# A gated mix of linear attention and a GEGLU on one core: three edits to a schedule written out by hand

## The chip, the cores and the metric

One core of a Trainium2 chip runs the whole program. The metric is the time of one execution in microseconds (us), the median of several runs. The core's engines each work through their own list of instructions in order: TensorE (PE, matmuls; its weight loads are shown apart as PEld), VectorE (DVE), ScalarE (ACT) and GpSimd (POOL). SyncE (SP) has a list that holds only DMA issues; ACT issues a few DMAs too. An instruction that waits holds up everything behind it in its list.

## The reference

The input x has S = 2048 tokens of D = 576 numbers; there are H = 32 heads of 18, and the hidden width of the feed-forward part is 4608.

```python
def _A_ref(x, wqkv, wo):                    # linear attention
    q, k, v = ...                           # from x @ wqkv
    phi = lambda t: jnp.where(t > 0, t + 1, jnp.exp(t)) + 1e-6
    pq, pk = phi(q), phi(k)
    kv = jnp.einsum("bhsd,bhse->bhde", pk, v)
    z = jnp.einsum("bhsd->bhd", pk)
    num = jnp.einsum("bhqd,bhde->bhqe", pq, kv)
    den = jnp.einsum("bhqd,bhd->bhq", pq, z)[..., None] + 1e-6
    return (num / den) ... @ wo
def _B_ref(x, w_gate, w_up, w_down):        # GEGLU
    h = _gelu(x @ w_gate) * (x @ w_up)
    return h @ w_down
g = _sigmoid((x * gate_w).sum(-1, keepdims=True))
return g * _A_ref(x, wqkv, wo) + (1 - g) * _B_ref(x, w_gate, w_up, w_down)
```

## The kernel before

**Numbers.** Matmuls run on fp32r operands. To keep float32 accuracy each operand is split in a high part (`ACTIVATE Copy` to fp32r on ACT) and the rest (a subtraction on DVE or POOL), and three of the four products of the parts are added in the same PSUM bank.

**Seven products in place of eight.** The three matrix products of the GEGLU go by 2x2 blocks with the seven products of Strassen's scheme. It needs four sums of blocks of x (S1 to S4, called x sums below), four of the weights (T1 to T4) and four of h.

**Stages of the program, in order of time.**

- Up to about 133 us: the key projection of 16 tiles of tokens (t = 0 to 15), its grams, and, in the gaps, the weights of queries (`w_part`, L150), of the first gate and up block (`Early`, stored to `wp_d`) and the x sums of the second half of the tokens: six pieces k, loaded to a buffer `xu` (`ahead_load`), summed on POOL (`ahead_sums`, L281), stored to `xsum_d` (`ahead_store`, L295).
- Up to about 286 us: states, queries (`query`, L414), denominators (`den`, L554, fed by `halves_of`, L544 and L545), their reciprocals by way of DRAM (`reciprocal` stores `rden_d`, L627; `reciprocals_load` brings it back spread over the heads, L631), `scale` (L643) and the output mixing (`mixed`, L662), whose result goes to `ga_d`.
- Up to 1108 us: 36 chains of gate and up products (`gu_steps`; the list is `CHAINS`). A chain is (p, n, m): half p of the tokens, block n of 18 of the hidden width, gate or up. It has 7 steps `s1`, `s6`, `s7`, `s5`, `s2`, `s4`, `s3`; each is a product of 7 matmuls (L798) followed by what DVE and ACT do with its bank. The first chain has the order s1, s6, s2, s7, s5, s4, s3, and its first four steps run inside the attention stage. There are eight banks, so PE may run ahead of DVE by a few products only. Chains are numbered c0, c1, ... below; c0 and c1 are gate and up of (0, 0), c2 and c3 of (0, 1), c4 is the gate of (1, 1), the first on the second half of the tokens; LAST-1 and LAST are the gate and up of (1, 0).
- To the end: the down product, 84 units of 36 matmuls (`unit`, L1066), whose banks DVE adds to accumulators `acc` (L1074). The accumulators start as the attention part, loaded from `ga_d` (`acc_load`, L1043). Blocks of h come back from DRAM (`h_load`, L967) and are split (`h_make`: ACT L972, DVE L973) into five buffers `hb`; blocks of the down weights are split by `d_make` (ACT L952, POOL L954) and summed by `d_sum` (POOL L959).

**Weights of a gate or up block.** `w_fetch` loads the raw block into `wraw` and makes the four sums T in `tsum` (POOL, L806); `wraw` and `tsum` are parts of one tile `stage`. `w_split`, a chain later, splits both into `W[m]` (tiles `wg`, `wu`) in two pieces: ACT L811, POOL L812 and L813, each for `wraw` and then for `tsum`; after it the next `w_fetch` is issued.

**What DVE does in a gate chain.** `s6` and `s7` make u2 and u3 (L847, L861), blocks 3, 2 and 1 are made by L833 and go through a gelu on ACT (L823); `s2` is a gelu straight from the bank (L853 for later chains). In an up chain L836 and L826 make h, and L875, L876, L877, L887 its sums, stored to `h_d` by SP (L829). `s1` copies its bank to p1 on ACT (L842); the next chain's p1 copy comes behind this chain's gelus in ACT's list, and the u2 of that chain waits for it.

**The order.** It is a schedule written out by hand: nothing reorders it. What is not a product is hung on the (chain, step) after which it is issued, by tables: `X_AT` (x parts from `xop_d`), `S_AT` (x sums k = 0 to 5: `s_make` splits a piece by ACT L988 and L989, which is on DVE for k < 4; `s_load` loads the next but one into the same half of the tile `f`, L983), `D_AT` and `H_AT`:

```python
    S_AT = [(0, 5), (1, 0), (2, 2), (2, 5), (3, 0), (3, 3)]
    H_AT = [(LAST - 1, 3), (LAST - 1, 6)]
            ...
            if (c, i) in H_AT:
                j = H_AT.index((c, i))
                h_make(j)
                h_load((2, 3)[j])
```

`stage` also holds the raw down weights (`draw`) of the last stage. Raw blocks of h arrive in `hraw` (two places before the down stage: a part of `xo` and `e123`).

Of the kernel before, what the change touches and what calls it, by code (L numbers as in the profile page):

```python
# [8 lines left out]
F32 = mybir.dt.float32  # L9
# [29 lines left out]
def tile_gated_mix(ctx, tc, xt, xs, xn, wk, wv, wq, wo, wgu, wdn, cst, out):  # L39
# [9 lines left out]
    xop_d = dram.tile([128, 3, 5, BS], F32, name="xop_d")  # L49
    xsum_d = [dram.tile([128, 4, 256], F32, name=f"xsum_d{k}") for k in range(6)]  # L50
    ga_d = [dram.tile([128, D], F32, name=f"ga_d{i}") for i in range(NST)]
    wp_d = [dram.tile([128, 7, 5, 128], F32, name=f"wp_d{m}") for m in range(2)]
    h_d = [[dram.tile([128, 7, 3, BS], F32, name=f"h_d{p}_{i}") for i in range(NF2 // 3)] for p in range(NP)]

# [218 lines left out]
    def do(n=1):  # L273
        for _ in range(n):
            todo.popleft()()
            load()

    def sum_blocks(raw, eng):
        a11, a12, a21, a22 = (raw[:, i] for i in range(4))
        eng.tensor_tensor(a22, a21, a22, OP.add)  # L280
        eng.tensor_tensor(a21, a11, a21, OP.subtract)  # L281
        eng.tensor_tensor(a11, a22, a11, OP.subtract)
        eng.tensor_tensor(a12, a12, a11, OP.subtract)
# [7 lines left out]
    def ahead_sums(k):  # L291
        sum_blocks(ahead[k], nc.gpsimd)

    def ahead_store(k):
        nc.sync.dma_start(xsum_d[k], ahead.pop(k))  # L295

    class Early:


# [9 lines left out]

        def make(self, part):  # L310
            if part < 2:
                b12, b11, b21, b22 = (self.raw[:, i] for i in range(4))
                t1, t2, t3, t4 = (self.sums[:, i] for i in range(4))
                for o, a, b in ((t1, b12, b11), (t2, b22, t1), (t3, b22, b12), (t4, b21, t2))[2 * part:2 * part + 2]:
                    nc.gpsimd.tensor_tensor(o, a, b, OP.subtract)
                return
            i, src = ((slice(0, 3), self.raw[:, 1:4]), (slice(3, 7), self.sums))[part - 2]
            nc.scalar.activation(self.hi[:, i], src, AF.Copy)
            if self.kt < 2:
                nc.gpsimd.tensor_tensor(self.lo[:, i], src, f32(self.hi[:, i]), OP.subtract)  # L320
            else:
                nc.gpsimd.tensor_tensor(self.hi[64:96, i], src[64:96], f32(self.hi[64:96, i]), OP.subtract)
            if part == 3:
                nc.sync.dma_start(wp_d[self.m][:, :, self.kt], f32(self.hi))
                if self.kt < 2:
                    nc.sync.dma_start(wp_d[self.m][:, :, 3 + self.kt], f32(self.lo))
# [32 lines left out]
    for t in range(FIRST, NST):  # L359
# [10 lines left out]
        for k, kt in enumerate((2, 3, 4) if t % 2 else (0, 1)):  # L370
# [3 lines left out]
            if k == (t == NST - 1):  # L374
                k_split(t)
                if now:
                    now.make(2)
                elif t == NST - 3:
                    ahead_sums(0)
                elif t == NST - 1:  # L380
                    ahead_sums(1)
                    ahead_store(0)
            if k == 1:
                xn_split(t)
# [304 lines left out]
    query(0, 0)  # L689
    query(0, 1)  # L690
    ahead_store(5)
    nc.sync.dma_start(xop_d[:, A22], f32(x_slot(3, 1)))
    den(3, 0)
    halves_of(3, 2)
    den(3, 1)
    halves_of(3, 3)
    query(0, 2)
    token_load(1)
    den(3, 2)
    halves_of(3, 4)  # L700
    den(3, 3)
    scaled(2, 0)
    query(0, 3)
    den(3, 4)
    scaled(2, 1)
    mixed(2, 0)
    reciprocals(3)
    query(0, 4)
    scaled(2, 2)
    token_sums(0, 0)  # L710
    mixed(2, 1)
# [2 lines left out]
    scaled(2, 3)  # L714
    token_sums(0, 1)
    query(1, 0)
    mixed(2, 2)
    den(0, 0)
    halves_of(0, 2)
# [80 lines left out]

    def w_fetch(n, m):
        nc.sync.dma_start(wraw, wgu[n, m])
        b12, b11, b21, b22 = (wraw[:, i] for i in range(4))
        t1, t2, t3, t4 = (tsum[:, i] for i in range(4))
        for o, a, b in ((t1, b12, b11), (t2, b22, t1), (t3, b22, b12), (t4, b21, t2)):
            nc.gpsimd.tensor_tensor(o, a, b, OP.subtract)  # L806

    def w_split(m):
        w = W[m]
# [104 lines left out]
    stage = stages.tile([128, 4320], F32, name="stage")  # L914
    e123 = stages.tile([128, 3, BS], F32, name="e123")
    wraw, tsum = (stage[:, c:c + 1536].rearrange("p (i k c) -> p i k c", i=4, k=3) for c in (0, 1536))
    w_fetch(1, 0)
    bothp = both.pool("both")
    X[1] = bothp.tile([128, 7, 5, BS], F32R, name="xo2")
    es += [e123[:, i] for i in range(3)]  # L920
# [52 lines left out]
            nc.vector.tensor_tensor(h[:, 1], raw, f32(h[:, 0]), OP.subtract)  # L973

    X_AT = {(0, 5): A11, (2, 2): A12, (3, 2): A22}
    S_AT = [(0, 5), (1, 0), (2, 2), (2, 5), (3, 0), (3, 3)]

    def s_raw(k):
        return f[:, k % 2 * 2:k % 2 * 2 + 2].rearrange("p a (b c) -> p (a b) c", b=2)
# [10 lines left out]

    for k in range(2):
        s_load(k)
    LAST = len(CHAINS) - 1
    D_AT = {(LAST - 2, 0): lambda: d_make(0, 0), (LAST - 2, 4): lambda: d_sum(T1), (LAST - 1, 0): lambda: d_sum(T2),
            (LAST - 1, 2): lambda: d_make(0, 1), (LAST - 1, 4): lambda: d_make(0, 2), (LAST - 1, 6): lambda: d_sum(T3),
            (LAST, 1): lambda: d_make(0, 3), (LAST, 4): lambda: d_sum(T4)}
    H_AT = [(LAST - 1, 3), (LAST - 1, 6)]
    at = {}
    for n in range(1, NF2):
        for m in range(2):  # L1000
# [1 line left out]
    for c, chain in enumerate(CHAINS):  # L1002
        for i, step in enumerate(first_steps if c == 0 else gu_steps(*chain)):
# [25 lines left out]
            if (c, i) in H_AT:  # L1029
                j = H_AT.index((c, i))  # L1030
                h_make(j)
                h_load((2, 3)[j])
    both.close()
    down = Scope()
    down.banks(8)
# [7 lines left out]
        nc.sync.dma_start(acc[p][:, 2 * i:2 * i + 2, j], ga_d[p * 8 + t].rearrange("p (n c) -> p n c", n=2))  # L1043

    h_load(4)
    for t in range(8):
        acc_load(0, t)

    C11, C12, C21, C22 = range(4)
# [28 lines left out]
    for u, (s, p, k) in enumerate(UNITS):  # L1078
        unit(u, 0)
        if u:  # L1080
            h_make(u + 3)
            h_load(u + 6)
        else:
            h_make(2)
            h_load(5)
        if 4 <= u < 8:
            acc_load(1, 2 * u - 8)
            acc_load(1, 2 * u - 7)
        unit(u, 1)
        if not u:  # L1090
            h_make(3)
            h_load(6)
        if u < 3:
            d_make(0, u + 4)
        if s < DG - 1:
# [72 lines left out]
```

## Time and profile before

| | us |
|---|---|
| median of 3 runs | 1517.13 (1515.93 to 1517.18) |
| the profiled execution's own time | 1516.98 |
| its span in the profile | 1515.2 |
| PE busy, share of the span | 1498.3, 99% |
| DVE busy | 1006.0, 66% |
| ACT busy | 546.6, 36% |
| POOL busy | 718.7, 47% |

The 1.8 us between the span and the profiled execution's time lie around the span. A profile line names the start, the duration, the engine and line, what is written and read, and in brackets the idle time of the engine just before and what ended it. Instructions of the same form that follow each other are put together (x7); the duration is then busy time. Matmuls overlap, so their ends are modelled.

### The profile page before, as it was taken

Reading aid. Unit: us, or ns where it says so; the run is one execution under the profiler, and the core shown is the slowest. Engines: PE = TensorE matmul, PEld = TensorE weight load, DVE = VectorE, ACT = ScalarE, POOL = GpSimd, SP = SyncE. Lnnn points to the kernel's source line nnn. Section 1 sums busy time; section 2 is a strip of 40 time slices with the busy share of each in tenths; the row PEclk is TensorE's granted clock in tenths of the full one; section 3 lists DMA queues with packets and bytes.
Section 4 is the critical chain, followed back from the end, with each engine's and each line's share of the span. In section 5 each row is a group of like instructions: output and inputs, shape, how many; then the busy total and the mean of one; then the engine's idle time right before and its main releaser. Section 6 shows DMA issues by size and latency. Waiting matters only on the chain.

```text
span 1515.2 us, 21583 instructions
## 1 busy us (share of the span) xinstructions
PE 1498.3 (99%) x8354; PEld 1322.1 (87%) x8354; DVE 1006.0 (66%) x1322; ACT 546.6 (36%) x711; POOL 718.7 (47%) x510
## 2 busy tenths in 40 slices
PE   9999999989999999999999999999999999999999
PEld 8998889877888888888888888888899999999999
DVE  7886776475665556665556665556678767777775
ACT  6554555323222332222332222332244344444431
POOL 2674512266545545545545545544347364644620
PEclk9999999999999999999999999999999999999999
DMA  7573354652332323332223332223878656565664
GB/s 246 160 209 117 144 217 168 242 225 91 139 119 91 107 102 139 139 118 91 104 104 139 140 118 91 104 105 119 309 261 290 214 167 213 168 214 174 207 199 135
DMA packets 95182, 244.00 MB, mean 161 GB/s; under 512 B 8928, under 2 KB 33144, under 8 KB 92648
## 3 DMA queue, kind: packets, MB, share of 16 engines
q1 hardware_dynamic: 92056, 230.77, 44.0%
q10 hardware_dynamic: 3024, 11.86, 2.1%
q8 instruction: 65, 1.06, 0.3%
q14 instruction: 37, 0.30, 0.1%
HBM read 155.15 MB, written 87.45 MB: 160 GB/s over the span
## 4 chain that ended last, share of the span: by engine, by line
PE 91%; DVE 3%; issue 2%; DMA 2%; ACT 1%; POOL 1%; SPq 0%; DVEq 0%; POOLq 0%; ACTq 0%
PE bank L798 52%; PE bank L1066 24%; PE pair L662 4%; PE bank L414 4%; PE pair L198 2%; PE kpair L243 2%; PE pair L243 2%; PE kpair L198 2%; PE den L554 1%; DMA stage<-wdn 1%; DMA xo<-h_d 1%; POOL wv L405 1%; DMA raw<-wk 0%; DMA acc<-ga_d 0%; DVE f L826 0%
## 5 line engine op out<-in xcount | busy, mean ns | idle before, releaser
L798 PE MATMUL bank<-xo,wg 128*128 128x512 f32 x1764 | 415.5, 395 | 4.6 <-DVE e L833 4.6
L798 PE MATMUL bank<-xo,wu 128*128 128x512 f32 x1764 | 414.3, 395 | 1.5 <-DVE p L836 1.5
L798 PEld LDWEIGHTS bank<-xo,wg 128*128 128x128 f32 x1764 | 333.1, 189 | 82.7 <-DVE e L833 5.5
L798 PEld LDWEIGHTS bank<-xo,wu 128*128 128x128 f32 x1764 | 333.3, 189 | 79.5 <-DVE p L836 1.9
L1074 DVE SCALAR_TENSOR_TENSOR acc<-bank,gate,acc 128x288 f32<-128x288 f32 x288 | 139.9, 512 | 68.6 <-PE bank L1066 66.5
L806 POOL TENSOR_TENSOR stage<-stage 128x384 f32<-128x384 f32 x136 | 161.2, 1205 | 41.4 <-DMA stage<-wgu 38.6
L842 ACT ACTIVATE p<-bank 128x512 f32<-128x512 f32 x72 | 43.1, 599 | 342.6 <-PE bank L798 342.6
L812 POOL TENSOR_TENSOR wg<-stage,wg 128x768 fp32r<-128x768 f32 (+1 forms) x34 | 74.0, 2177 | 188.9 <-ACT wg L811 181.0
L812 POOL TENSOR_TENSOR wu<-stage,wu 128x768 fp32r<-128x768 f32 (+1 forms) x34 | 81.2, 2388 | 144.7 <-ACT wu L811 143.4
L1066 PE MATMUL bank<-xo 128*128 128x288 f32 x1044 | 141.6, 295 | 1.5 <-DVE acc L1074 1.5
L1066 PEld LDWEIGHTS bank<-xo 128*128 128x128 f32 x1044 | 139.5, 188 | 1.9 <-DVE acc L1074 1.8
L954 POOL TENSOR_TENSOR xo<-stage,xo 128x432 fp32r<-128x432 f32 x44 | 64.6, 1490 | 101.2 <-ACT xo L952 99.1
L847 DVE TENSOR_TENSOR u<-bank,p 128x512 f32<-128x512 f32 x72 | 49.5, 687 | 94.8 <-PE bank L798 91.9
L954 POOL TENSOR_TENSOR wd<-stage,wd 128x432 fp32r<-128x432 f32 x40 | 58.8, 1494 | 106.5 <-ACT wd L952 106.5
L1066 PE MATMUL bank<-wd,xo 128*128 128x288 f32 x792 | 106.5, 294 | 0.0
L1066 PEld LDWEIGHTS bank<-wd,xo 128*128 128x128 f32 x792 | 105.3, 188 | 0.0
L833 DVE TENSOR_TENSOR f<-bank,u 128x512 f32<-128x512 f32 x54 | 37.3, 692 | 76.6 <-PE bank L798 76.2
L833 DVE TENSOR_TENSOR e<-bank,u 128x512 f32<-128x512 f32 x54 | 37.1, 691 | 75.0 <-PE bank L798 74.9
L823 ACT ACTIVATE f<-f 128x512 f32<-128x512 f32 x54 | 34.2, 633 | 138.0 <-DVE f L833 138.0
L959 POOL TENSOR_TENSOR stage<-stage 128x432 f32<-128x432 f32 x48 | 76.3, 1614 | 0.0
L861 DVE TENSOR_TENSOR u<-bank,u 128x512 f32<-128x512 f32 x72 | 49.8, 692 | 36.9 <-PE bank L798 34.8
L823 ACT ACTIVATE e<-e 128x512 f32<-128x512 f32 x54 | 34.2, 633 | 95.4 <-DVE e L833 95.4
(188 smaller groups left out, 2309.6 us busy)
## 6 DMA issues: line engine op xcount, KB each, us to landing
h_d<-sx SPq DMA_DIRECT2D x108, 256.0 KB, 7.5
stage<-wgu SPq DMA_DIRECT2D x34, 768.0 KB
xo<-h_d SPq DMA_DIRECT2D x29, 768.0 KB, 4.3
e<-h_d SPq DMA_DIRECT2D x28, 768.0 KB, 4.3
hraw<-h_d SPq DMA_DIRECT2D x27, 768.0 KB
h_d<-e SPq DMA_DIRECT2D x72, 256.0 KB, 2.1
h_d<-f SPq DMA_DIRECT2D x72, 256.0 KB, 2.1
stage<-wdn SPq DMA_DIRECT2D x6, 1728.0 KB, 8.3
```

The source lines that it names most:

```text
L198: nc.tensor.matmul(out_t[:, :n], xa, kvw[i][:rows, r, lo:lo + n], start=(k == 0), stop=(k == 13))
L243: nc.tensor.matmul(y[:, n, :KH], a, p[:, n * KH:(n + 1) * KH], start=(k == 0), stop=(k == len(ops) - 1))
L414: nc.tensor.matmul(ps[:R], qw[i][:rows, rw, GO[g]:GO[g] + R], xa, start=(k == 0), stop=(k == 13))
L798: nc.tensor.matmul(ps, w_, x_, start=start and i == 0, stop=i == 6, skip_group_check=not start)
L806: nc.gpsimd.tensor_tensor(o, a, b, OP.subtract)
L812: nc.gpsimd.tensor_tensor(w[:, i, 3:5], src[:, :, 0:2], f32(w[:, i, 0:2]), OP.subtract)
L823: nc.scalar.activation(es[i], es[i], AF.Gelu_apprx_tanh)
L833: nc.vector.tensor_tensor(es[i], a, b, OP.add)
L954: nc.gpsimd.tensor_tensor(w[:, 1, c], src[:, c], f32(w[:, 0, c]), OP.subtract)
L959: nc.gpsimd.tensor_tensor(draw[:, o, c], draw[:, x, c], draw[:, y, c], OP.subtract)
L1066: nc.tensor.matmul(y, h[:, hl, g, t * 128:(t + 1) * 128], w[:, wl, g * 288:(g + 1) * 288], start=k in (1, 5) and n == 0, stop=n == len(ops ...
L1074: nc.vector.scalar_tensor_tensor(o, y, gate[:, 1, st:st + 1], o, op0=OP.mult, op1=OP.add)
```

## The change

Three places of the program are edited.

1. **x sums in the key projection.** `ahead_sums(1)` is issued in tile 14 in place of tile 15.
2. **The first gate chains.** The table `S_AT` of the x-sum splits is moved. The weight sums of the second up block (1, UP) are no longer made by `w_fetch` on POOL in chain c1; they are made in the attention stage, by 12 smaller POOL instructions on pieces loaded into three `xu` buffers, stored to a new DRAM tile `ws_d` and loaded from there into `tsum`. `w_fetch(1, 0)` is issued behind the loads of the first two x sums.
3. **The entry of the down stage.** `H_AT` has a third place, so that three blocks of h are made in chain LAST-1 and `h_load(5)` is issued there; ahead of the first unit four accumulators are loaded instead of eight, the other four in unit 0, and those of the second half of the tokens at units 4, 5, 7, 8 instead of 4 to 7.

```diff
+    ws_d = dram.tile([128, 4, 3, 128], F32, name="ws_d")
+    def weight_sums(raw, out, parts=slice(0, 4)):
+        b12, b11, b21, b22 = (raw[:, i] for i in range(4))
+        t1, t2, t3, t4 = (out[:, i] for i in range(4))
+        for o, a, b in ((t1, b12, b11), (t2, b22, t1), (t3, b22, b12), (t4, b21, t2))[parts]:
+            nc.gpsimd.tensor_tensor(o, a, b, OP.subtract)
...
+    def up_view(kt):
+        return ahead[6 + kt].rearrange("p a (b c) -> p (a b) c", b=2)
+    def up_load(kt):
+        ahead[6 + kt] = xup.tile([128, 4, 256], F32, name="xu")
+        nc.sync.dma_start(up_view(kt)[:, :4], wgu[1, 1, :, :, kt])
+    def up_sums(kt):
+        v = up_view(kt)
+        weight_sums(v[:, :4], v[:, 4:])
+    def up_store(kt):
+        nc.sync.dma_start(ws_d[:, :, kt], up_view(kt)[:, 4:])
...
                 elif t == NST - 3:
                     ahead_sums(0)
+                elif t == NST - 2:
+                    ahead_sums(1)
                 elif t == NST - 1:
-                    ahead_sums(1)
                     ahead_store(0)
...
     ahead_store(5)
+    up_load(0)
+    up_load(1)
+    up_load(2)
     nc.sync.dma_start(xop_d[:, A22], f32(x_slot(3, 1)))
...
     query(0, 2)
+    up_sums(0)
     token_load(1)
...
     query(0, 3)
+    up_sums(1)
+    up_store(0)
...
     reciprocals(3)
     query(0, 4)
+    up_sums(2)
+    up_store(1)
...
     query(1, 0)
+    up_store(2)
...
     def w_fetch(n, m):
         nc.sync.dma_start(wraw, wgu[n, m])
...
+        if (n, m) == (1, 1):
+            nc.sync.dma_start(tsum, ws_d)
+        else:
+            weight_sums(wraw, tsum)
...
-    w_fetch(1, 0)
...
-    S_AT = [(0, 5), (1, 0), (2, 2), (2, 5), (3, 0), (3, 3)]
+    S_AT = [(0, 4), (0, 5), (2, 4), (2, 6), (3, 1), (3, 3)]
...
     for k in range(2):
         s_load(k)
+    w_fetch(1, 0)
...
-    H_AT = [(LAST - 1, 3), (LAST - 1, 6)]
+    H_AT = [(LAST - 1, 1), (LAST - 1, 3), (LAST - 1, 5)]
...
-                h_load((2, 3)[j])
+                h_load((2, 3, 5)[j])
...
     h_load(4)
-    for t in range(8):
+    for t in range(4):
         acc_load(0, t)
...
             h_load(u + 6)
         else:
-            h_make(2)
-            h_load(5)
-        if 4 <= u < 8:
-            acc_load(1, 2 * u - 8)
-            acc_load(1, 2 * u - 7)
-        unit(u, 1)
-        if not u:
             h_make(3)
             h_load(6)
+            for t in range(4, 8):
+                acc_load(0, t)
+        if u in (4, 5, 7, 8):
+            t = 2 * (u - 4 - u // 7)
+            acc_load(1, t)
+            acc_load(1, t + 1)
+        unit(u, 1)
```

The order of PE's instructions is the same in both programs. Line numbers of the changed kernel are higher by 19 to 28 from the attention stage on.

On DVE, chains c0 to c2, before (L833, L847, L861 and L836 take banks; L989 is an x-sum split):

```order
L833 TENSOR_TENSOR e_3175<-bank,u_2850 128x512 x2
L989 TENSOR_TENSOR xo_3184<-f,xo_3184 128x4x256
L833 TENSOR_TENSOR e_3175<-bank,u_2849 128x512
L989 TENSOR_TENSOR xo_3184<-f,xo_3184 128x4x256
L847 TENSOR_TENSOR u_2849<-bank,p_2848 128x512
...
L861 TENSOR_TENSOR u_2850<-bank,u_2849 128x512
L989 TENSOR_TENSOR xo_3184<-f,xo_3184 128x4x256
L833 TENSOR_TENSOR e_3175<-bank,u_2850 128x512 x2
L989 TENSOR_TENSOR xo_3184<-f,xo_3184 128x4x256
L833 TENSOR_TENSOR e_3175<-bank,u_2849 128x512
```

The same stretch of DVE in the changed kernel, where L833 is L861, L847 is L875, L861 is L889 and L989 is L1016:

```order
L861 TENSOR_TENSOR e_3197<-bank,u_2872 128x512
L1016 TENSOR_TENSOR xo_3201<-f,xo_3201 128x4x256
L861 TENSOR_TENSOR e_3197<-bank,u_2872 128x512
L1016 TENSOR_TENSOR xo_3201<-f,xo_3201 128x4x256
L861 TENSOR_TENSOR e_3197<-bank,u_2871 128x512
...
L889 TENSOR_TENSOR u_2872<-bank,u_2871 128x512
L861 TENSOR_TENSOR e_3197<-bank,u_2872 128x512
L1016 TENSOR_TENSOR xo_3201<-f,xo_3201 128x4x256
L861 TENSOR_TENSOR e_3197<-bank,u_2872 128x512
L861 TENSOR_TENSOR e_3197<-bank,u_2871 128x512
L1016 TENSOR_TENSOR xo_3201<-f,xo_3201 128x4x256
```

Splits 0 and 1 each stand one block earlier, both inside c0; in c2 the first of them stands behind block 3 instead of ahead of it, the second behind block 1.

On ACT, chain LAST-1 to the start of LAST, before (L972 is the first half of `h_make`, L952 that of `d_make`, L842 the copy of p1 of chain LAST):

```order
L816 DMA wu<-wp_d_96 128x4480
L952 ACTIVATE xo<-stage 128x864
L823 ACTIVATE f<-f 128x512
L972 ACTIVATE xo<-xo 128x1536
L853 ACTIVATE f<-bank 128x512
L952 ACTIVATE xo<-stage 128x864
L823 ACTIVATE f<-f 128x512 x2
L972 ACTIVATE xo<-e_3175 128x1536
L842 ACTIVATE p_2848<-bank 128x512
```

The same in the changed kernel (L999 for L972, L979 for L952, L851 for L823, L870 for L842):

```order
L844 DMA wu<-wp_d_97 128x4480
L999 ACTIVATE xo<-xo 128x1536
L979 ACTIVATE xo<-stage 128x864
L851 ACTIVATE f<-f 128x512
L999 ACTIVATE xo<-e_3197 128x1536
L881 ACTIVATE f<-bank 128x512
L979 ACTIVATE xo<-stage 128x864
L851 ACTIVATE f<-f 128x512
L999 ACTIVATE xo<-xo 128x1536
L851 ACTIVATE f<-f 128x512
L870 ACTIVATE p_2870<-bank 128x512
```

A third L999 now stands ahead of the last gelu of LAST-1 and ahead of the p1 copy of LAST.

On SP, in the attention stage, the changed kernel (before, the rows on `ws_d` and `xu<-wgu` are not there):

```order
L302 DMA xsum_d_78<-xu 128x1024
L309 DMA xu<-wgu 128x4x128 x3
L714 DMA xop_d<-xo 128x2560
L616 DMA xc<-xs 128x2048
L316 DMA ws_d<-xu 512x1x128
L646 DMA rden_d_70<-rb 35x256
L646 DMA rden_d_71<-rb 35x256
L650 DMA rb<-rden_d_70 126x1x1280
L650 DMA rb<-rden_d_71 126x1x1280
L316 DMA ws_d<-xu 512x1x128 x2
L616 DMA xc<-xs 128x2048
```

Three loads of 256 KB and one store now stand ahead of the two stores of reciprocals (L646, before L627), two stores behind their loads.

More of the change, by code (lines that the diff above doesn't have):

```diff
@@ L311, in make @@
             if part < 2:
[L312 to L315, printed above, removed]
+                weight_sums(self.raw, self.sums, slice(2 * part, 2 * part + 2))
                 return
```

4 lines of the change are left out of this document (removed).

## The prediction

> **What bounds the kernel now.** I read the page's busy times first, then the waits of PE, then the timeline around each wait.
>
> ```profile
> PE 1498.3 (99%) x8354; PEld 1322.1 (87%) x8354; DVE 1006.0 (66%) x1322; ACT 546.6 (36%) x711; POOL 718.7 (47%) x510
> PE bank L798 <- DVE e L833: 4.6, 2, 4.1
> PE bank L1066 <- DVE acc L1074: 2.4, 2, 1.5
> PE bank L798 <- DVE p L836: 1.5, 1, 1.5
> PE bank L414 <- DVE qw L150: 1.1, 1, 1.1
> ```
>
> PE is the bound: 1498.3 of a span of 1515.2 us. The change leaves its list as it is, so it can gain only what PE waits for (total, times, longest), and what a slow clock stretches. The four rows are the four places that the edits touch: 9.6 us together. The timeline of chains c0 to c4 shows the largest.
>
> ```profile
> 291.57 1.23 DVE L989 TENSOR_TENSOR xo<-f,xo 128x1024 fp32r<-128x1024 f32 x1 [1.65 <-ACT xo L988]
> ...
> 294.45 2.53 ACT L811 ACTIVATE wg<-stage 128x1152 fp32r<-128x1152 f32 x2
> ...
> 297.96 1.78 DVE L989 TENSOR_TENSOR xo<-f,xo 128x1024 fp32r<-128x1024 f32 x1 [4.56 <-ACT xo L988]
> ...
> 301.99 1.89 PE L798 MATMUL bank<-xo,wu 128*128 128x512 f32 x7 [1.50 <-DVE p L836]
> 302.06 1.76 POOL L813 TENSOR_TENSOR wg<-stage,wg 32x512 fp32r<-32x512 f32 x1
> 303.71 9.84 PE L798 MATMUL bank<-xo,wg 128*128 128x512 f32 x42
> 303.89 5.84 POOL L806 TENSOR_TENSOR stage<-stage 128x384 f32<-128x384 f32 x4
> 313.27 0.69 DVE L861 TENSOR_TENSOR u<-bank,u 128x512 f32<-128x512 f32 x1
> 313.54 2.34 POOL L812 TENSOR_TENSOR wu<-stage,wu 128x1024 fp32r<-128x1024 f32 x1
> 313.88 3.08 DVE L989 TENSOR_TENSOR xo<-f,xo 128x1024 fp32r<-128x1024 f32 x1
> 316.88 1.28 DVE L833 TENSOR_TENSOR e<-bank,u 128x512 f32<-128x512 f32 x2
> 317.61 3.35 PE L798 MATMUL bank<-xo,wg 128*128 128x512 f32 x7 [4.07 <-DVE e L833]
> 320.77 12.35 PE L798 MATMUL bank<-xo,wu 128*128 128x512 f32 x49
> 332.95 11.64 PE L798 MATMUL bank<-xo,wg 128*128 128x512 f32 x49
> 316.00:320.00 4.00, 2.39 (x6) 1.90 (x7) 2.16 (x3) 2.41 (x4) 3.53 (x3) 0.50 0.99 407
> ```
>
> The split L989 at 313.88 took 3.08 us beside POOL's L812, where its fellow took 1.23, and stood ahead of block 3 (L833), whose bank PE wanted: 4.07. The last row is a stretch of time: busy time of PE, PEld, DVE, ACT and POOL, the granted clock, the DMA share and GB/s. In 316 to 320 the clock was 0.50.
>
> **The change part by part.** The sum is made against the profiled execution's 1516.98, which is 0.15 under the median of the runs.
>
> *x sums a tile earlier.*
>
> ```profile
> 116.47 0.75 DVE L150 TENSOR_TENSOR qw<-raw,qw 32x576 fp32r<-32x576 f32 x1
> 121.69 1.14 POOL L281 TENSOR_TENSOR xu<-xu 128x256 f32<-128x256 f32 x1
> 124.09 1.30 DVE L150 TENSOR_TENSOR qw<-raw,qw 32x576 fp32r<-32x576 f32 x1
> ```
>
> The L150 on which PE waits 1.1 ran 1.30, where one without POOL sums beside it ran 0.75; what DVE did ahead of it ran beside the same sums. They now stand a tile earlier, so L150 comes at least 0.55 earlier, and about that again for what is ahead. I take a gain of 0.9 (0, if the wait moves with the sums, to 1.1, the whole wait).
>
> *Weight sums in attention.*
>
> ```profile
> L315 POOL TENSOR_TENSOR er<-er x24: 452/467/996, 38.8 to 101.1; 128x128 f32<-128x128 f32 x24
> xsum_d<-xu SPq DMA_DIRECT2D x6, 512.0 KB, 10.8
> 186.21 1.15 SPq L295 DMA_DIRECT2D xsum_d<-xu  x1
> 198.95 2.33 SPq L627 DMA_DIRECT2D rden_d<-rb  x2
> 206.45 1.61 SPq L631 DMA_DIRECT2D rb<-rden_d  x2
> 211.26 5.54 POOL L604 TENSOR_TENSOR xo<-xc,xo 128x512 fp32r<-128x512 f32 x4 [26.79 <-ACT xo L601]
> 216.15 1.32 DVE L643 SCALAR_TENSOR_TENSOR r<-r,rb 126x640 f32<-126x640 f32 x1
> 220.86 1.09 PE L554 MATMUL den<-hl,zmk 126*128 126x512 f32 x4
> ```
>
> The first row gives the shortest, median and longest of such instructions in ns; the second the KB and the median time from issue to landing. The 12 POOL instructions, 12 x 0.467 = 5.6 us, lie in POOL's idle 26.79 and cost nothing there; without that cover they would be 5.6 on POOL only. The price is in SP's list: the third load needs the `xu` of the last x-sum store, which by the median landing of 10.8 is free at about 197 to 199, and then a `ws_d` store waits for POOL's sums. The reciprocals' stores behind it go out 4 to 6 us after their 198.95, so the loads (206.45 before) end near 216 to 217, just when DVE wants them for L643 (216.15). PE needs what follows L643 for the denominators at 220.86. L643 could be about a us late before PE notices. I take a loss of 0.3 (0 to 2: nothing is taken out here, so there is no gain, and 6 late at most leaves no more behind the slack).
>
> *First gate chains.* Before, three things were lost: 1.50 and 4.07 of waits, and the slow clock behind the second: the seven matmuls from 317.61 to 320.77 took 3.16 instead of 11.64 / 7 = 1.66, and the next chain 12.35 instead of 11.64. That makes 1.5 + 0.7 = 2.2, in all 7.8.
>
> After: the L989 of 297.96 is out of the way of chain c1, so the 1.50 goes. In c2 block 3 stands ahead of the split. Its L833 follows L861 at 313.27 + 0.69 and ends at 314.65. PE was ready at 317.61 - 4.07 = 313.54, so about 1.1 is left, and less where DVE, freed of 1.50 before, runs earlier. POOL's four sums of 5.84 ahead of the up split go too (a load from `ws_d` takes their place), so L812 of 313.54 need no longer meet the split.
>
> What is late next is the split of `wg`. ACT's L811, at 294.45 before, now has both x-sum splits ahead of it with their gelus, and DVE in between: I add 2.7 us (one split of 1.04 on ACT and one of 1.23 on DVE with a gelu behind). POOL's split then ends not at 302.06 + 1.76 = 303.82 but at 305.6 to 306.4. Chain c2 starts at 303.71 - 1.50 = 302.2 and its second product, on T2, wants the last piece at the 14th matmul, 302.2 + 13 x 0.2376 (11.64 / 49) = 305.3. That is a wait of 0.4 to 1.2. Together I keep 1.6 of waits (0 to 3.5) and take a gain of 7.8 - 1.6 = 6.2. None of them is as long as 4.07, so I take the clock to stay at full.
>
> *Entry of the down stage.*
>
> ```profile
> 1087.38 0.33 ACTq L816 DMA_DIRECT2D wu<-wp_d  x1
> 1091.00 0.32 SPq L829 DMA_DIRECT2D h_d<-sx  x1
> DMA to landing us min/median/max: 7.5/7.5/7.5
> 1095.23 1.76 DVE L973 TENSOR_TENSOR xo<-xo 128x1536 fp32r<-128x1536 f32 x1 [2.08 <-ACT xo L972]
> 1096.96 11.64 PE L798 MATMUL bank<-xo,wu 128*128 128x512 f32 x49
> 1099.18 1.47 ACT L972 ACTIVATE xo<-e 128x1536 fp32r<-128x1536 f32 x1
> 1100.56 0.57 ACT L842 ACTIVATE p<-bank 128x512 f32<-128x512 f32 x1
> ...
> 1127.19 1.49 ACT L972 ACTIVATE xo<-xo 128x1536 fp32r<-128x1536 f32 x1 [6.91 <-DMA xo<-h_d]
> ...
> xo<-h_d SPq DMA_DIRECT2D x29, 768.0 KB, 4.3
> ```
>
> The two waits of the down stage, 2.4, follow from blocks of h that come late: one behind eight accumulator loads (6.91 on ACT), one behind a load of down weights for which ACT's list stands still. With one block more in stock, and four loads moved, both go: 2.4 (0 to 2.4).
>
> The new wait is on ACT in LAST-1: the third L972 needs a block whose load is issued on SP behind the `h_d` stores. The last of these, issued at 1091.00, landed after 7.5 (the third row is the answer for it alone), at 1098.5, with the load of `wu` (1087.38) beside it; the block lands some 2 later, at 1100.5 (1097.4 to 1102.8). Behind the L972 in ACT's list stand the last gelu of LAST-1 and the p1 copy of LAST (1100.56 before), and DVE's L973 stands ahead of the block that this gelu needs: 1100.5 + 1.47 + 1.76 + 0.69 + 0.63 (L833 and a gelu) + 0.57 = 1105.7. PE reaches the product that adds to that bank (the fifth) at 1096.96 + 4 x 1.66 = 1103.6. I take a wait of 2.2 (0 to 4.5). The edit nets -0.2 (-2.4 to +2.1).
>
> By the rows alone a wait of 1.50 left the clock at full and one of 4.07 halved it; 2.2 lies between. If it halved, 2.2 more would be lost, and the sum would be 1512.2; it is nearer to 1.50, so I take none. The Trainium skill, "TensorE: Matmul & The Clock Gate", section "Part 1: The HAM clock gate (the "warmup" mystery)", puts the fall behind an idle window of about 3.4 us: by that rule too 2.2 costs no clock. No row here shows the threshold itself.
>
> Sum: -0.9 + 0.3 - 6.2 - 0.2 = -7.0. Forecast: 1516.98 - 7.0 = **1510.0**.
>
> **The rivals.** *R1, the third block comes in time.* If the store's 7.5 does not hold back the load behind it, so that the block moves beside the `wu` load, there is no new wait: 1510.0 - 2.2 = 1507.8. Against it speaks that very store. The Trainium skill, "DMA: Bandwidth & Descriptors", section "Queues, rings and completion order", says that an engine takes turns between queues packet by packet; the 7.5 beside `wu` shows small turns at best. 0.16.
>
> *R2, the `wg` split is later still.* If ACT's chain through both splits meets POOL at the shared work as L989 did (3.08 instead of 1.23), the residual is 3.5 to 4.5 in place of 1.6: 1512 to 1513. 0.15.
>
> *R3, no change.* The waits come back elsewhere: residual 3.5, B's 2, D's 2.1, A's 0: 1516.98 - 4.3 + 2 + 2.1 = 1516.8. It needs all bad ends at once, or one unseen wait of 7 us. 0.11.
>
> *R4, slower: the `ws_d` load comes late.* It can go out only after POOL has split the old `tsum`, at about 306, and all of SP waits with it. If it takes the 10.8 of the `xsum_d` stores or more and lands at 318, the up split (ACT, then POOL, 4 us) ends at 322, and chain c3, starting at 302.2 + 11.64 + 1.6 = 315.4, wants it in its second product, 315.4 + 1.66 = 317.1. With the stretch of the clock (2.2) and the splits behind it that is 5 + 2.2 = 7 lost there, and half of it again at c4, whose weights go through the same `stage`: 1510.0 + 7 + 3.5 = 1520.5. It decides once the load takes more than 8 us from issue. Against it: it is 768 KB, and loads of h of that size landed in 4.3 in the median. 0.11.
>
> *The change does not do what it says*: excluded, the order on DVE, ACT and SP shows each move.
>
> **How the numbers follow.** Forecast 0.47, R1 0.16, R2 0.15, R3 0.11, R4 0.11. About 0.2% (3.0 us) is what a measurement of this kernel can tell from no change. Faster (below 1513.95): the forecast, R1 and R2, 0.77 after a hundredth for their tails; the same: R3 with it, 0.12; slower (above 1520.0): R4, 0.11. The range holds the forecast, R1, R2 and part of R3. Low: all good ends, -1.1 - 7.0 (residual 0.8) - 2.1 = -10.2, 1506.8. High: 1515.0, where residual, B and D are each near their bad ends but A holds.
>
> **What would show it.** Right: in the waits of PE after, neither the 4.1 on L833 nor the 1.1 on L150, nor the 2.4 of the down stage; a granted clock of 1.00 in 316 to 320; a wait of ACT for `xo<-h_d` at about 1097 and of PE on p1 at about 1103; some tenths for POOL's `wg` split near 305. Wrong: a wait of over 3 us in c2 to c4, a clock of 0.50 there, SP stuck before the reciprocals so that PE waits for L643's followers near 221, or a landing of `stage<-ws_d` over 8 us after its issue.

## The result and the profile after

The changed kernel takes 1514.91 us (median of 12 runs), the kernel before 1516.81 in the same comparison: a ratio of 0.9988, 95% interval 0.9976 to 1.0, that is 1.8 us less (0 to 3.6). Single runs spread from 1511.6 to 1520.3 here and from 1515.2 to 1521.0 before, so one profile is one draw: the profiled execution of the changed kernel took 1517.68, 2.8 above its median, and its span is 0.7 us longer than that of before.

The waits of PE in the changed kernel:

```profile
PE bank L826 <- DMA wu<-wp_d: 2.4, 1, 2.4
PE pair L681 <- ACT p L68: 2.1, 1, 2.1
PE bank L826 <- DVE e L861: 1.5, 2, 0.8
PE bank L1094 <- DVE u L864: 1.3, 1, 1.3
...
PE bank L826 <- ACT p L870: 0.5, 1, 0.5
PE den L573 <- DVE hl L564: 0.4, 1, 0.4
...
PE bank L826 <- POOL wg L841: 0.2, 1, 0.2
```

All four rows on which the forecast rested are gone: no 4.1 on L833 (now L861, 0.8 at most), no 1.5 on L836, no 1.1 on L150, no 2.4 of the accumulators. Others have come, three of which no step of the prediction has: 2.4 on the load of `wu`, 2.1 on p (L68) in the mixing, 1.3 on u (L864) at the first down units. Stretches of the same kernel (busy time of PE, PEld, DVE, ACT, POOL, granted clock, DMA share, GB/s):

```profile
276.00:280.00 4.00, 1.85 (x14) 1.62 (x13) 1.07 (x2) 1.01 (x2) 0.00 (x0) 1.00 0.94 363
280.00:284.00 4.00, 3.94 (x18) 3.71 (x18) 2.15 (x3) 1.10 (x2) 0.00 (x0) 0.58 0.71 282
316.00:320.00 4.00, 3.19 (x14) 2.56 (x14) 1.78 (x3) 2.06 (x3) 3.62 (x2) 1.00 1.08 432
1092.00:1096.00 4.00, 2.36 (x11) 1.55 (x9) 1.76 (x1) 2.86 (x4) 1.06 (x1) 1.00 0.94 357
1096.00:1100.00 4.00, 3.25 (x8) 2.63 (x9) 0.69 (x1) 0.63 (x1) 3.50 (x4) 0.57 0.81 298
```

In 316 to 320 the clock is full, where it was 0.50. It is halved now behind both new waits: 0.58 in 280 to 284, 0.57 in 1096 to 1100.

As PE's order is the same in both programs, the same matmul can be set beside itself. After minus before, in the two profiles: -2.0 at 125 us (0.6 of it from the first 10 us), -0.4 at 247, +3.8 at 280 behind the first new wait and its slow clock, -2.7 at 322 behind the first gate chains, +1.3 at 1099 behind the wait on `wu` and its slow clock, +3.6 at 1111, +0.6 at 1149 and to the end. The gate chains brought 6.5; the two new waits with their clock took 4.1 and 4.0. Another 1.7 went between 221 and 247, at the third reciprocals, of which the table of waits shows only 0.4:

```profile
203.72 1.01 SPq L646 DMA_DIRECT2D rden_d<-rb  x2
...
217.39 0.83 DVE L662 SCALAR_TENSOR_TENSOR r<-r,rb 126x640 f32<-126x640 f32 x1 [1.71 <-DMA rb<-rden_d]
...
220.50 0.50 PE L573 MATMUL den<-hl,zmk 126*128 126x512 f32 x1 [0.45 <-DVE hl L564]
```

The stores of these reciprocals go out 4.8 later than before (198.95), as the prediction worked out, and DVE has them 1.2 later (216.15 before).

The timeline of the changed kernel at the first new wait:

```profile
266.38 0.76 SPq L650 DMA_DIRECT2D rb<-rden_d  x1
267.24 11.23 SPq L1010 DMA_DIRECT2D f<-xsum_d  x2
267.86 0.33 ACTq L928 DMA_DIRECT2D wu<-wp_d  x1
278.13 0.83 DVE L662 SCALAR_TENSOR_TENSOR r<-r,rb 126x640 f32<-126x640 f32 x1 [5.27 <-DMA rb<-rden_d]
279.78 10.07 PE L681 MATMUL pair<-kw,p 126*128 126x288 f32 x60 [2.15 <-ACT p L68]
```

The same places of before:

```profile
266.30 0.75 SPq L631 DMA_DIRECT2D rb<-rden_d  x1
268.11 0.33 ACTq L900 DMA_DIRECT2D wu<-wp_d  x1
275.76 0.82 DVE L643 SCALAR_TENSOR_TENSOR r<-r,rb 126x640 f32<-126x640 f32 x1 [2.65 <-DMA rb<-rden_d]
281.15 0.85 SPq L983 DMA_DIRECT2D f<-xsum_d  x2
```

The last load of reciprocals (`rb`, issued at 266.3 before and 266.4 after) is there for DVE at 275.76 before and at 278.13 after. Two things stand beside it in the changed kernel: the load of the up weights of c1 (`wu`, in both), and the first of the two x-sum loads (`f`). It went out 14 us later before, since `w_fetch(1, 0)` ahead of it in SP's list waited for `stage`. The change moved `w_fetch` behind these loads, and so set the first one free. The second did not come with it: the row joins two issues, and the second one went out at 278.12, when the reciprocals had landed.

### The profile page after: what moved, and what is told of

The parts are those of the page before. It is cut to its first block, busy times and chain, and to the rows that moved or that the text cites. A ratio compares the mean times of both kernels' runs of the same rounds, so it can differ in the third digit from the quotient of the medians.

```text
span 1515.9 us, 21599 instructions
## 1 busy us (share of the span) xinstructions
PE 1500.4 (99%) x8354; PEld 1322.2 (87%) x8354; DVE 1005.8 (66%) x1322; ACT 546.1 (36%) x711; POOL 719.7 (47%) x518
## 4 chain that ended last, share of the span: by engine, by line
PE 84%; DVE 5%; DMA 4%; issue 3%; POOL 2%; ACT 2%; SPq 0%; ACTq 0%; DVEq 0%; POOLq 0%
PE bank L826 50%; PE bank L1094 26%; PE pair L199 2%; PE kpair L244 1%; PE pair L244 1%; PE bank L433 1%; PE kpair L199 1%; DMA rb<-rden_d 1%; DMA rden_d<-rb 1%; DMA xsum_d<-xu 1%; DMA xo<-h_d 1%; DVE f L854 1%; PE pair L681 1%; POOL wv L424 1%; DMA xu<-wgu 0%
## 5 line engine op out<-in xcount | busy, mean ns | idle before, releaser
L283 POOL TENSOR_TENSOR stage<-stage 128x384 f32<-128x384 f32 x132 | 155.4, 1197 | 42.8 <-DMA stage<-wgu 40.3
L870 ACT ACTIVATE p<-bank 128x512 f32<-128x512 f32 x72 | 43.0, 597 | 332.4 <-PE bank L826 332.4
L875 DVE TENSOR_TENSOR u<-bank,p 128x512 f32<-128x512 f32 x72 | 49.5, 688 | 94.2 <-PE bank L826 88.8
L861 DVE TENSOR_TENSOR e<-bank,u 128x512 f32<-128x512 f32 x54 | 37.1, 691 | 75.8 <-PE bank L826 75.6
L861 DVE TENSOR_TENSOR f<-bank,u 128x512 f32<-128x512 f32 x54 | 37.3, 692 | 75.3 <-PE bank L826 73.1
L851 ACT ACTIVATE f<-f 128x512 f32<-128x512 f32 x54 | 34.2, 632 | 142.5 <-DVE f L861 142.5
L889 DVE TENSOR_TENSOR u<-bank,u 128x512 f32<-128x512 f32 x72 | 49.8, 692 | 35.8 <-PE bank L826 33.7
L681 PEld LDWEIGHTS pair<-kw,p 126*128 126x128 f32 (+1 forms) x480 | 66.6, 193 | 5.0 <-ACT p L68 3.1
```

Of the source, the lines that this page charges most:

```text
L681: nc.tensor.matmul(y[:, i, :288], p[:R, a, g], KW[g][:R, wl, i * 288:(i + 1) * 288], start=(n == 0), stop=(n == 14))
L861: nc.vector.tensor_tensor(es[i], a, b, OP.add)
L875: nc.vector.tensor_tensor(u2, b, p1, OP.add)
L889: nc.vector.tensor_tensor(u3, c, u2, OP.add)
```

## The experiments

Each was measured beside the kernel before on the same chip. The table puts the ratio's distance from 1 in us (of 1517).

| run | edits in it | ratio, 95% interval | us against before |
|---|---|---|---|
| the change | all | 0.9988, 0.9976 to 1.0 | -1.8 |
| e1 | all, but `w_fetch` first | 0.9990, 0.9978 to 1.0003 | -1.5 |
| e2 | all, but the old entry | 1.0006, 0.9996 to 1.0016 | +0.9 |
| e3 | `w_fetch` late alone | 1.0013, 1.0003 to 1.0024 | +2.0 |
| e4 | first h block early alone | 1.0014, 1.0004 to 1.0024 | +2.1 |
| e5 | moves of the x sums alone | 0.9966, 0.9952 to 0.9979 | -5.2 |
| e6 | moves and `ws_d` | 0.9984, 0.9974 to 0.9994 | -2.4 |
| e7 | new entry alone | 0.9990, 0.9981 to 0.9998 | -1.5 |
| e8 | e6, third h block in LAST | 0.9990, 0.9980 to 1.0001 | -1.5 |
| e9 | moves and new entry | 0.9973, 0.9963 to 0.9984 | -4.1 |
| e10 | moves, `ws_d` made but not used | 1.0009, 0.9999 to 1.0018 | +1.4 |
| e11 | e6, `ws_d` work later | 0.9979, 0.9965 to 0.9992 | -3.2 |
| e12 | all, load of c1's `wu` later | 0.9986, 0.9976 to 0.9996 | -2.1 |
| e13 | e5, load of c1's `wu` later | 0.9970, 0.9960 to 0.9979 | -4.6 |
| e14 | e6, load of c1's `wu` later | 0.9973, 0.9963 to 0.9983 | -4.1 |
| e15 | e11, load of c1's `wu` later | 0.9968, 0.9954 to 0.9982 | -4.9 |

**e1: `w_fetch` first again.**

```diff
+    w_fetch(1, 0)
     bothp = both.pool("both")
...
     for k in range(2):
         s_load(k)
-    w_fetch(1, 0)
```

> The changed kernel with one edit undone: w_fetch(1, 0) stands ahead of the loads of the first two x sums again. Theory 1 (those loads, no longer held behind w_fetch, go out 14 us earlier and share the DMA engines with the last reciprocals' load, on which PE waits at 279.8): the wait of 2.15 and the slow clock behind it go, 4.1 us, so about 1510.8 median. Rival 1 (the ws_d traffic of the attention stage makes the last reciprocals late): the wait stays, within 0.5 us of the changed kernel.

Its profile bears theory 1 out, with a wait of 0.8 instead of 2.1 on p, and a span of 1510.8; the median does not, 1517.03 over ten runs. The profiled execution was the shortest of the ten. One profile is not enough here.

**e2: the old entry.** The part of the diff on `H_AT`, `acc_load` and the units is undone.

> The changed kernel with the entry of the down stage as before (two blocks of h made in LAST-1, eight accumulator loads). Theory 2 (the load of the third block, now issued before wu has landed, shares the engines with the load of wu): the wait of 2.39 on wu, the slow clock behind it (1.5), the 0.47 and the 1.32 go, the old waits of 2.4 come back: 3.3 us faster, about 1511.6 median. Rival 2 (wu is late because the chains now come 2.8 us earlier than its load can): the wait on wu stays at 2 or more.

The expected 3.3 did not come: 2.7 slower than the change in the ratios. The wait on `wu` was there, 1.5, without a third block, and so were one of 4.9 on p and two of 1.8 and 0.4 at the third reciprocals.

**e3: `w_fetch` late, in the kernel before.**

> The kernel before with only this: w_fetch(1, 0) behind the loads of the first two x sums. Theory 1: a wait on the last reciprocals of about 2 us with a slow clock behind it appears, 3 to 4 us slower than before, or 1 to 2 at the least, since attention is less late here. Rival 1: no change, within 0.5 us.

Slower by 2.0, and the wait on p is there:

```profile
267.28 10.39 SPq L982 DMA_DIRECT2D f<-xsum_d  x2
268.07 0.33 ACTq L900 DMA_DIRECT2D wu<-wp_d  x1
277.33 0.82 DVE L643 SCALAR_TENSOR_TENSOR r<-r,rb 126x640 f32<-126x640 f32 x1 [4.26 <-DMA rb<-rden_d]
278.98 8.57 PE L662 MATMUL pair<-kw,p 126*128 126x288 f32 x60 [1.12 <-ACT p L67]
```

So the order of `w_fetch` alone costs; the wait and what follows it put PE 1.6 later by 286 us. But this profile also has a wait of 2.07 on `wu` at the start of LAST, with the entry as before:

```profile
PE bank L798 <- DMA wu<-wp_d: 2.1, 1, 2.1
```

**e4: the first block of h early, in the kernel before.**

```diff
-    H_AT = [(LAST - 1, 3), (LAST - 1, 6)]
+    H_AT = [(LAST - 1, 1), (LAST - 1, 6)]
```

> The kernel before with only the first block of h made two steps earlier in LAST-1, so that the next load of h (768 KB) goes out at about 1091 instead of 1097; no third block. Theory 2: PE waits for wu by 2 to 3 us at the start of LAST, with a slow clock behind it: 3 to 4 us slower. Rival 2: no wait for wu, within 0.5 us of before.

No wait for `wu` in its profile; slower by 2.1 all the same. The profile shows that much in the down stage: PE waits 0.7 more on the accumulators, and behind the second of these waits (1.83, where before had 1.55) the granted clock is 0.60 in 1148 to 1152, where it was 1.00. Against before, PE loses 2.1 between 1111 and 1160. Theory 2 falls: the wait on `wu` appears without an early load of h (e2, e3) and fails to appear with one (e4, and e7 below). Over all seventeen profiles it is there in seven (0.5 to 2.4), with and without the third block. In these seven the load landed 10.2 to 12.1 us after its issue, in the other ten 9.0 to 9.3. What makes it late in some executions is open.

**e5: the moves of the x sums alone.**

```diff
+                elif t == NST - 2:
+                    ahead_sums(1)
                 elif t == NST - 1:
-                    ahead_sums(1)
...
-    S_AT = [(0, 5), (1, 0), (2, 2), (2, 5), (3, 0), (3, 3)]
+    S_AT = [(0, 4), (0, 5), (2, 4), (2, 6), (3, 1), (3, 3)]
```

> The kernel before with two moves of x sums alone: the table S_AT of the change, and ahead_sums(1) in tile 14. No ws_d, no new order of w_fetch, the old entry. Theory 3 (the gain in the first gate chains and the key projection is real and comes from these moves; what ate it are the other edits): the waits of 1.5 on L836 and 1.1 on L150 go, the 4.1 shrinks below 2 and the slow clock with it, 4 to 6 us faster, about 1512. Rival 3 (the gain needs the weight sums out of POOL's way): L989 still meets POOL, the 4.1 becomes a wait elsewhere, not more than 2.5 us faster.

5.2 faster (3.2 to 7.3): theory 3 holds. The weight sums are still on POOL, and they cost what the waits and the timeline show, no more:

```profile
315.62 2.99 DVE L990 TENSOR_TENSOR xo<-f,xo 128x1024 fp32r<-128x1024 f32 x1 [2.20 <-ACT xo L989]
...
319.80 6.50 PE L799 MATMUL bank<-xo,wu 96*128 96x512 f32 x27 [1.03 <-POOL wu L814]
```

The split still meets POOL (2.99), but no block of PE's waits behind it now; PE waits 1.03 for the up split instead of 4.07 for a block. This kernel beats the one before beyond its interval, and by the ratios it is 3.3 faster than the change, with intervals that overlap slightly (it has only five executions).

**e6: moves and `ws_d`.** e1's order and the old entry.

> The changed kernel with w_fetch(1, 0) ahead of the x-sum loads and with the old entry of the down stage; the ws_d sums stay. Theory 3: as the kernel with the x-sum moves alone, less what the ws_d traffic costs in attention (1 to 2): 3 to 5 us faster than before, about 1513. Rival 3: over 1 us faster than the kernel with the x-sum moves alone.

2.4 faster than before, less than the 3 to 5 expected, so `ws_d` takes back 2.7 of the 5.2. Its profile has one of the two longest waits on p (4.75; e2 has 4.9):

```profile
266.69 0.76 SPq L650 DMA_DIRECT2D rb<-rden_d  x1
267.32 0.33 ACTq L928 DMA_DIRECT2D wu<-wp_d  x1
...
279.76 0.83 DVE L662 SCALAR_TENSOR_TENSOR r<-r,rb 126x640 f32<-126x640 f32 x1 [7.89 <-DMA rb<-rden_d]
281.41 8.80 PE L681 MATMUL pair<-kw,p 126*128 126x288 f32 x51 [4.75 <-ACT p L68]
```

Here the load of `wu` goes out 0.63 us behind that of the reciprocals (1.81 before), and DVE gets them 13.1 us after issue (9.5 before). The x-sum loads are not in it: they went out at 285.

**e7: the new entry alone.**

> The kernel before with the new entry of the down stage alone. By the prediction's own term -0.2 (-2.4 to +2.1). Theory 4 (the third block costs two new waits, on p1 in LAST of 1 to 2 us and on u of 1.3 in the first down units, and takes away the two of 2.4): 0 to 1 us slower. Rival 4 (it is also what makes wu late): a wait for wu of 2 us or more, 3 to 5 us slower.

1.5 faster (0.3 to 2.9), where theory 4 had 0 to 1 slower, and no wait for `wu`. The wait on p1 is the one that the prediction worked out:

```profile
1099.93 1.49 ACT L972 ACTIVATE xo<-xo 128x1536 fp32r<-128x1536 f32 x1 [0.87 <-DMA xo<-h_d]
1101.45 2.17 DVE L973 TENSOR_TENSOR xo<-xo 128x1536 fp32r<-128x1536 f32 x1 [3.05 <-ACT xo L972]
1103.54 0.68 DVE L833 TENSOR_TENSOR f<-bank,u 128x512 f32<-128x512 f32 x1
1104.26 0.63 ACT L823 ACTIVATE f<-f 128x512 f32<-128x512 f32 x1 [2.83 <-DVE f L833]
1104.79 0.58 ACT L842 ACTIVATE p<-bank 128x512 f32<-128x512 f32 x1
...
1105.42 5.18 PE L798 MATMUL bank<-xo,wu 128*128 128x512 f32 x21 [2.08 <-ACT p L842]
```

The stretch behind that wait in the same kernel, with the clock third from the end:

```profile
1104.00:1108.00 4.00, 2.58 (x11) 2.13 (x12) 2.58 (x5) 1.93 (x3) 1.74 (x2) 1.00 0.62 203
```

**e8: the third block in LAST.** e6's order, `H_AT` with (LAST - 1, 3), (LAST - 1, 6), (LAST, 3).

> The changed kernel with w_fetch(1, 0) ahead of the x-sum loads, and with the three blocks of h made later: at steps 3 and 6 of LAST-1 as before, the third at step 3 of LAST. Theory 4: no wait for the load of the third block, so the p1 wait goes and the old waits of 2.4 in the down stage stay away: 1 to 3 us faster than the changed kernel with both edits undone. Rival: DVE's split of the third block delays the blocks of LAST, a wait there of 1 to 2 us takes its place: the same as with both undone.

The rival holds as to the place: the p1 wait is gone, one of 2.5 on u (L864) at the first down units stands in its place. It is 1.5 faster than before, 0.9 slower than e6.

**e9: moves and new entry.**

> The kernel before with the moves of the x sums and the new entry of the down stage; neither the ws_d sums nor the new order of w_fetch. Theory 5 (the four edits add: moves -5.1, ws_d sums +2.7, entry -1.5, order of w_fetch +2.0, together the -1.9 of the change): -6.6, a ratio of 0.9957. Rival 5 (the entry gains nothing once the chains come earlier): as the moves alone, -5.1 or less.

Rival 5: 4.1 faster, not 6.6. In its profile the p1 wait is 2.2 and a wait of 1.3 on u follows, which e7 does not have; together they are more than the 2.3 on the accumulators that the entry removes from e5.

**e10: `ws_d` made but not used.** e6 with `w_fetch` making every block's sums on POOL.

> The moves of the x sums, and the loads, sums and stores of ws_d in the attention stage, but w_fetch makes the sums on POOL as before: the work on ws_d is done and its result not used. Theory 6 (the price of the ws_d edit lies in the attention stage, on SP and the DMA engines): +2.7 over the moves alone, a ratio of 0.998 to 0.9985. Rival 6 (the price lies in chain c1, where the load of ws_d holds up SP and the splits): as the moves alone, 0.9966.

Theory 6 holds, and more strongly than it said: 6.5 slower than e5. Against e6 it would put the use of `ws_d` at 3.8 of gain, where the profiles show 1.3 (between 324 and 330 us, in the times of before, PE loses 1.3 against before in e5 and e10, and nothing in e6); the rest is inside the two intervals or was not found.

**e11: `ws_d` later.** The loads stand behind `reciprocals(3)` and `query(0, 4)`, the sums behind `query(1, 0)`, the stores behind `token_load(2)`.

> As the changed kernel with both other edits undone (moves of the x sums and ws_d sums), but the three loads of up weights are issued behind the third pair of reciprocals' loads, the sums behind the first query of the second token quarter, the stores behind the load of the next tokens. Theory 7 (the price comes from SP standing ahead of the reciprocals): their stores go out as early as before and the price falls from 2.7 to below 1: a ratio of 0.9966 to 0.997. Rival 7 (the price is the traffic itself, 2.3 MB more on busy DMA engines, wherever it stands): 0.998 to 0.999.

3.2 faster than before: 2.0 behind e5, 0.8 ahead of e6, with intervals that overlap. It settles nothing by its time.

**e12: the load of c1's up weights one tile later, in the changed kernel.**

```diff
-    nc.scalar.dma_start(f32(W[1]), wp_d[1])
     first_steps[3]()
     for t in range(BT):
...
         mixed(1, t)
+        if t == 0:
+            nc.scalar.dma_start(f32(W[1]), wp_d[1])
```

> The changed kernel with one move: the load of the up weights of c1 (2240 KB, on ACT's queue) is issued one token tile later in the last mixing, about 6 us. Theory 8 (the last reciprocals' load, on which PE waits near 279, is late because this load shares the DMA engines with it): that wait goes, the load of the reciprocals takes 7 to 8 us instead of 11.7, 1.5 to 3 us faster than the changed kernel, a ratio of 0.997 to 0.998. Rival 8 (the early x-sum loads alone make it late): the load still takes over 10 us, no gain.

The place behaves as theory 8 says, though the first x-sum load still goes out early:

```profile
267.71 0.77 SPq L650 DMA_DIRECT2D rb<-rden_d  x1
268.57 6.67 SPq L1011 DMA_DIRECT2D f<-xsum_d  x2
274.90 0.82 DVE L662 SCALAR_TENSOR_TENSOR r<-r,rb 126x640 f32<-126x640 f32 x1 [1.26 <-DMA rb<-rden_d]
275.60 0.45 ACTq L934 DMA_DIRECT2D wu<-wp_d  x1
```

DVE has the reciprocals 7.2 us after issue instead of 11.8, and PE waits no more on p (L68). The time hardly follows: 2.1 faster than before against 1.8.

**e13, e14, e15: the same move in e5, e6 and e11.**

> The moves of the x sums alone, and the load of the up weights of c1 one token tile later. Theory 9 (the last reciprocals' load loses to that load on the DMA engines): the load takes 7 to 8 us, the wait of 1.0 on it goes, 1 us faster than the moves alone: a ratio of 0.996. Rival 9 (c1 now waits for its weights): 1 us or more slower than the moves alone.

> The moves of the x sums and the ws_d sums as in the change (old entry, w_fetch ahead of the x-sum loads), and the load of the up weights of c1 one token tile later. Theory 9 (most of the price of the ws_d edit is that it makes the last reciprocals' load meet that load): the price falls from 2.7 to below 1, a ratio of 0.996 to 0.997, as the moves alone. Rival 9b (the price lies in the third reciprocals, near 221, or in the traffic): 0.998 to 0.999, as without this move.

> The same with the ws_d loads, sums and stores behind the third reciprocals. Theory 9: no price is left, and the gain of the ws_d sums in chain c1 (1.0 to 1.3 in the profiles) is added: a ratio of 0.995 to 0.996, faster than the moves alone. Rival 9b: 0.998.

In none of the four profiles with the later load does PE wait on p (L68); of the other thirteen it waits in ten, 0.5 to 4.9. But in all four PE then waits 1.1 to 1.2 on p1 in chain c1, which none of the others does by more than 0.4: there is part of rival 9 in it. e13 gains nothing on e5 (0.9970, 0.9966). e14 gains on e6: 0.9973 against 0.9984, medians 1512.63 and 1515.75. The price of `ws_d` falls from 2.7 (e6 against e5) to 0.5 (e14 against e13). That is as theory 9 has it, though the two intervals touch. e15 has no price left either, and its 0.9968 does not beat e5.

**The same stretches in all the profiles.** As PE's order is the same in every kernel here, its matmuls can be set beside those of before in each profile. The table has what PE loses (+) or gains (-) in three stretches, in the times of before: at the third reciprocals, at the last ones, and in c0 and c1.

| profiles | 221 to 247 | 274 to 286 | 286 to 302 |
|---|---|---|---|
| before's own order: e4, e7 | 0.0, 0.0 | -0.1, -0.1 | 0.0, 0.0 |
| `w_fetch` late alone: e3 | 0.0 | 1.6 | 0.0 |
| moves: e5, e9 | 0.0, 0.0 | 1.5, 1.0 | -1.6, -1.5 |
| moves and `ws_d`: e1, e6, e8, e10 | 0.7, 0.6, 4.2, 0.4 | 1.3, 6.7, 1.3, 2.1 | -1.3, -1.7, -1.1, -1.3 |
| the same and `w_fetch` late: the change, e2 | 1.7, 3.3 | 4.1, 7.4 | -1.7, -1.8 |
| moves, `ws_d` later: e11 | 0.0 | 1.1 | -1.1 |
| load of `wu` later: e12, e13, e14, e15 | 2.6, 0.0, 0.6, 0.3 | -0.1 in all | -0.3, -0.4, -0.4, -0.3 |

`ws_d` costs at the third reciprocals wherever its work stands ahead of them, 0.4 to 4.2, and nothing is lost there without it. At the last reciprocals the moves, `ws_d` and the order of `w_fetch` each go with a larger loss in the mean, and the later load of `wu` takes all of it away; the wait on p1 takes back 1 us or so in the next stretch. Kernels that are the same up to a stretch (e1, e6 and e8) differ there by up to 5.4, so a row of one or two profiles gives no price.

## Why the prediction was wrong, point by point

**x sums a tile earlier: right.** The 1.1 on L150 is in no profile of a kernel with this edit. In all thirteen PE gains 1.4 at this place against before, more than the 0.9 (0 to 1.1) of the forecast.

**First gate chains: right.** Forecast -6.2. In the two profiles PE gains 6.5 between 280 and 322 us; what is left there is 0.8 on L861 and 0.15 for the `wg` split, and the clock stays full. Together with the x sums the forecast was -7.1; e5, which has these two moves alone, measures -5.2 (-7.3 to -3.2). That the weight sums had to leave POOL for it, as the working had it, is not borne out: e5 keeps them there, and PE waits 1.03 for them.

**Weight sums in attention: the step that failed.** Forecast a loss of 0.3, at most 2; e6 against e5 measures 2.7, which their intervals leave uncertain by some 2.5 either way (an estimate from the two). The profiles show it at two places. At the third reciprocals the working had the mechanism and not the size: the stores went out 4.8 later in the change, inside its 4 to 6, but the slack of about a us that it gave PE behind L643 was not there. PE lost 0.4 to 4.2, 1.8 in the mean of the eight profiles with this work ahead of the reciprocals. And the working stopped there. It did not ask what a stage that runs closer to its transfers does at the last reciprocals, the next use of the same path, where a 2240-KB load on another queue follows within 2 us: there 1.3 to 6.7 was lost with `ws_d`, against 1.0 and 1.5 with the moves alone. That loss is gone with the later load of `wu`, and the price falls to 0.5 (e14 against e13).

**`w_fetch` behind the x-sum loads: a step that is missing.** The order was shown, and no term of the sum was given to it. It took away what held the x-sum loads back, and the first of them joined the last reciprocals' load. Alone, in e3, it measures +2.0 (0.5 to 3.6), of which its one profile has 1.6 at this place; the rest of what that profile loses is on `wu` and the accumulators.

**Entry of the down stage: right alone.** Net -0.2 (-2.4 to +2.1) was forecast; e7 measures -1.5 (-2.9 to -0.3). A wait of 2.2 on p1 was forecast and 2.08 measured. The working's own terms (1100.5 and five more) add up to 1105.6, not 1105.7, so they give 2.0. On top of the moves it gains nothing (e9 against e5: +1.1), since a wait on u follows: between 1099 and 1111 PE loses 2.3 in e7 and 4.1 in e9, and behind that the entry brings 3.0 in both.

**The clock.** The forecast took a wait of 2.2 to leave it full. In e7 it does: 2.08, clock 1.00 in the stretch behind. In the changed kernel waits of 2.15 and 2.39 were followed by 0.58 and 0.57, which cost about 2.0 and 1.6 on top of the waits; in e4 a wait of 1.83 was followed by 0.60. The rule of the Trainium skill ("TensorE: Matmul & The Clock Gate", "Part 1: The HAM clock gate (the "warmup" mystery)"), an idle window of about 3.4 us, was read there as a bound, and the measurement says that it is none. Its remark that the window runs freely is in accord with one length of wait going both ways.

The clock is also part of what moves single runs. In e11 the three shortest executions (1510.3 to 1510.8 us) had a mean granted clock of 1.000, the four longest (1517.8 to 1518.7) one of 0.997 or 0.998; 0.0025 of 1516 us is an estimated 3.8 of the 7.6 us between them. In the mean of their runs the change and before both have 0.998, e5, e13, e14 and e15 0.9995 or more: by the same estimate 2.3 us of what these four gain.

**The rivals.** None of them was it. R2 and R4 were about chains c2 and c3, which went as forecast: the `ws_d` load landed within 5.2 us of its issue (309.11, ACT's split at 314.30). R3 asked for an unseen wait of 7 us; there were two, of 4 each with their clock in the profile, at places without a term.

**The range.** It reaches to 1515.0, and the median of 1514.91 lies just inside. That is luck: the high end was made up of the gate chains, `ws_d` and the entry each near its bad end. Of these only `ws_d` went that way; the losses at the last reciprocals and on `wu` were no part of it. The low end is called all good ends, but takes 2.1 for the entry, whose good end is 2.4.

**How far it adds up.** Alone or one upon the other: moves -5.2, `ws_d` +2.7, entry -1.5, order +2.0 make -2.0, and the change measures -1.8. But the pairs do not add: the entry is worth -1.5 alone, +1.1 on e5, +0.9 on e6 (e1); the order is worth +2.0 alone, +3.3 on e6 (e2), -0.3 on e1 (the change). So how much of the loss is the order's and how much the entry's remains open, and so does the rest of what moves single runs by some us. That e4, which moves one place in a table, measures +2.1 shows that a price of 2 can come from one wait with a slow clock behind it.

## What to carry to other kernels

A load that is held back behind a blocked issue is doing the transfers beside it a service: before moving the blocker, look up what its followers will meet. When an edit adds traffic to a stage, follow it to the last transfer on which the bound engine waits, not only to the first, and look at large loads on the other queue. Where single runs spread by more than the effect, take the price of an edit from runs with that edit alone, and use the profiles, more than one, for the mechanism.

## What the runs showed of the hardware

The last reciprocals' load (630 KB) landed 5.9 to 7.2 us after its issue in the four profiles in which the 2240-KB load of the other queue went out 7 to 9 us behind it, and 7.0 to 13.7 in the thirteen in which it went out 0.6 to 1.8 behind. The distance is not all: it took 7.0 to 9.4 in before, e4 and e7, which are the same program up to there, 10.3 and 10.8 with the moves of the x sums (e9, e5), 10.2 to 13.0 with `ws_d` besides, 10.9 with `w_fetch` late alone, and 11.7 and 13.7 with all three, at distances of 0.6 to 1.8. The Trainium skill ("DMA: Bandwidth & Descriptors", "Queues, rings and completion order") says that an engine takes turns between queue rows packet by packet, and these numbers are in accord with it: in e6 the 2240-KB load went out 0.6 behind the reciprocals' and landed 0.6 ahead of it (279.1 and 279.7). Of waits of nearly one length some were followed by a clock near half (1.83 in e4, 2.15 and 2.39 in the changed kernel) and some were not (2.08 in e7, 2.07 in e3).
